# Batch 0's h w2 - h w1 accumulated in PSUM from fp16 weights, w1 w_out made ahead of the first row phase, the full-precision weights loaded behind batch 1's x, and three lines of batch 1's schedule moved

## The chip, the cores and the metric

One core of one Trainium2 chip. The time is the device time of one execution in microseconds (us). "Full clock" below means a mean granted clock of 0.998 to 1.0 over the execution, "low clock" 0.988 to 0.995.

In the lines of the profile PE is TensorE and PEld its weight loads, DVE is VectorE, ACT ScalarE, POOL GpSimd, SP SyncE, and SPq the queue of DMAs that SyncE issues. x9 is a count, and [1.05 <-ACT hwd L474] says that the engine had been idle for 1.05 us until that instruction of ScalarE ended. A chunk is 128 rows of x, an evacuation is the copy of a finished result out of PSUM, a filler is a matmul whose result nobody reads, and a DMA lands when its transfer is complete.

## The reference, cut to what matters

```python
# x: (4, 12544, 128), inducing: (32, 128), w1, w2: (128, 1024), w_out: (1024, 128)
def mab(q, kv):
    s = scale * (q @ kv.transpose(0, 2, 1))
    s = s - s.max(-1, keepdims=True)
    a = np.exp(s)
    a /= a.sum(-1, keepdims=True) + 1e-09
    return a @ kv
h = mab(I, x)            # 32 inducing points look at all 12544 rows, per batch
y = mab(x, h)            # each row looks at the 32 points
# then, per row of y:
g = np.maximum(y @ w1, y @ w2)
out = g @ w_out
```

The kernel uses max(h1, h2) = h1 + relu(h2 - h1). For each batch it therefore needs two small matrices once h is known: hwd = h (w2 - w1), 32 x 1024, which feeds the relus, and m1 = h (w1 w_out), 32 x 128, which feeds the linear part. It needs w1out = w1 w_out for the latter.

## The kernel before

Batch 0 is read and reduced first (the run-up, to about 30 us), because nothing else can start before its h. Then the row phases of batch 0 run, and the pool steps of batch 1 (transposing x, scores, exp, accumulation) are slotted in between, at fixed counts of finished chunks. The same happens for batches 2 and 3.

The weights before: four pieces in full precision, then w1 and w_out in fp16, all in front of x of batch 1 on GpSimd's queue. GpSimd subtracts w1 from w2, which gives w21.

```python
for h in range(2):
    sl = slice(512 * h, 512 * (h + 1))
    nc.gpsimd.dma_start(out=w2f[:, sl], in_=moe_w2[:, sl])
    nc.gpsimd.dma_start(out=w1f[:, sl], in_=moe_w1[:, sl])
nc.gpsimd.dma_start(out=w1h, in_=moe_w1)
nc.gpsimd.dma_start(out=woutp, in_=moe_w_out.rearrange("(jb j) c -> j jb c", j=128))
# ... cut ...
def small_hwd(b, halves=(0, 1)):
    # ... cut: per half of 512 columns ...
    nc.tensor.matmul(out=ps, lhsT=st[b]["hT4"], rhs=w21[:, sl], start=True, stop=True)
    # half 0 is copied by VectorE, half 1 by ScalarE, with rw as the factor for batch 0
```

The end of the run-up, in the order of issue. `fill` issues matmuls on a constant tile; `phase` is one row phase (four matmul groups of 32 rows, then a relu for each); `stage` makes the exp that a block's phases need; weights_2 transposes w1h into w1T (copies by VectorE and ScalarE), weights_3 multiplies w1T and woutp.

```python
for i in range(3):
    load_x(1, i)
weights_1()
weights_1b(nc.gpsimd, slice(512, 1024))
for i in range(3, 7):
    load_x(1, i)
sums = small_h(0)
fill(4)
small_sums(*sums)
stage(blocks[0])
# rw on VectorE
small_hwd(0, (0,))
# ... cut: definitions ...
phase(plan_phase(False))      # first phase
small_hwd(0, (1,))
weights_2()
phase(plan_phase(False))      # second phase
stage(blocks[1])
weights_3()
# ... main loop
```

The schedule of the pool steps. The scores of unit u end in an exp that writes the tile eu; there are NEU = 5 such buffers and 6 units. A DMA transposition on SP's queue (pool_turn) turns eu into eT, and the accumulation reads eT. x itself is transposed into xT on the same queue, in which the stores of the output go too.

```python
t_first, t_step = (8, 2.2) if b == 1 else (-6, 3.4)
for u in range(NU):
    if b == 1:
        s, turn, acc = 24 + 5 * u, 45 + 1.5 * u, 56 + 2 * u
    else:
        s = turn = 9 + 9 * u
        acc = s + 10
    at(base + int(s), pool_scores, b, u)
    at(base + int(turn), pool_turn, b, u)
    at(base + int(acc), pool_accum, b, u)
# ... cut ...
for j in range(14):
    at(base + int(t_first + t_step * j), transpose_x_dma, b, j)
# ... and where a scores or accumulation job may be issued:
late = jobs and chunks_done[0] >= due[jobs[0]] + 4
if jobs and (ck.mode == "col" or len(jobs) > 1 or late):
```

The softmax here doesn't subtract the row's maximum and nothing guards it: scores larger than these inputs give would overflow.

## Time and profile before

| | us |
|---|---|
| median of 3 runs | 337.24 (336.65 to 337.7) |
| the execution that was profiled | 336.5, span 334.4, granted clock 1.000 |
| PE busy | 323.9, 97% of the span |

The median is that of all executions; the profile is one execution. The lines that carry the reading (two stretches in which TensorE waits, 25 to 35 us and 70 to 75 us, in a kernel in which it otherwise hardly waits) are shown in the prediction.

### The profile page before, as it was taken

What the parts mean: (1) busy time and instruction counts of PE and PEld (TensorE: products, weight loads), DVE (VectorE), ACT (ScalarE), POOL (GpSimd) and SP (SyncE); (2) the same over time, 40 slices, a digit from 0 to 9 for tenths busy, and PEclk for the clock granted to TensorE, in tenths of its full rate; (3) what the DMA queues carried; (4) which work ended last, traced back from release to release, by engine and by line L of the source; (5) the groups of instructions that cost most, each with busy time, mean ns of one, the idle gap of its engine ahead of it and who ended that gap; (6) DMA issues with size and microseconds to landing.
All of it is one profiled execution on the core that took longest, in us unless ns stands there. A gap on an engine that the chain in (4) does not pass through costs nothing.

```text
span 334.4 us, 12588 instructions
## 1 busy us (share of the span) xinstructions
PE 323.9 (97%) x5403; PEld 243.5 (73%) x5403; DVE 286.1 (86%) x532; ACT 278.9 (83%) x549; POOL 24.0 (7%) x51
## 2 busy tenths in 40 slices
PE   7987999989999999999999999999999999999995
PEld 3774777757777777777777777777778777777785
DVE  2247999969988999998999999999999989999873
ACT  2558899968688989999888899888879999999961
POOL 7272000000220000000040000000000000000000
PEclk9999999999999999999999999999999999999999
DMA  7999999994299999984279999995222222222233
GB/s 131 211 260 213 200 175 206 204 193 126 64 215 247 245 188 175 167 176 136 84 159 243 237 210 194 187 183 160 86 90 97 82 97 97 86 106 90 77 121 112
DMA packets 70104, 52.93 MB, mean 158 GB/s; under 512 B 52097, under 2 KB 54561, under 8 KB 70049
## 3 DMA queue, kind: packets, MB, share of 16 engines
q1 hardware_dynamic: 64368, 37.71, 47.8%
q0 software_dynamic: 5680, 14.42, 22.1%
q8 instruction: 42, 0.69, 0.9%
q14 instruction: 14, 0.11, 0.1%
HBM read 27.80 MB, written 25.69 MB: 160 GB/s over the span
## 4 chain that ended last, share of the span: by engine, by line
PE 87%; DMA 6%; DVE 2%; ACT 1%; issue 1%; POOL 1%; SPq 1%; DVEq 0%; POOLq 0%; ACTq 0%
PE ps L769 57%; PE ps L930 21%; DMA xn<-in_x_dram 3%; PE ps L574 2%; PE ps L365 2%; PE ps L317 1%; DMA xT<-xn 1%; DVE relu L949 1%; DMA eT<-eu 1%; SPq L171 1%; PE ps L240 1%; POOL xn L165 1%; PE ps L614 1%; PE ps L463 0%; DVE o L796 0%
## 5 line engine op out<-in xcount | busy, mean ns | idle before, releaser
L946 ACT ACTIVATE relu<-ps 128x512 f16<-128x512 f32 x459 | 243.7, 602 | 31.5 <-PE ps L930 23.8
L949 DVE TENSOR_SCALAR relu<-ps 128x512 f16<-128x512 f32 x325 | 208.3, 681 | 21.7 <-PE ps L930 20.2
L769 PE MATMUL ps<-woutp,relu 128*128 128x128 f16 x3136 | 217.9, 220 | 0.0
L769 PEld LDWEIGHTS <-relu 128*128 128x128 f16 x3136 | 177.1, 98 | 39.7 <-issue 29.3
L930 PE MATMUL ps<-e,hwd 32*128 32x512 f16 (+2 forms) x880 | 89.2, 360 | 2.2 <-ACT hwd L474 1.1
L796 DVE TENSOR_TENSOR o<-ps,rp 128x512 f32<-128x512 f32 (+3 forms) x108 | 68.4, 635 | 5.5 <-PE ps L769 3.2
L930 PEld LDWEIGHTS <-hwd 32*128 32x128 f16 x880 | 24.8, 91 | 24.8 <-issue 2.6
L930 PE MATMUL ps<-m,e 32*128 32x128 f16 x381 | 38.8, 217 | 0.8 <-ACT eu L328 0.7
L930 PEld LDWEIGHTS <-e 32*128 32x128 f16 x381 | 21.5, 92 | 3.6 <-issue 0.9
L165 POOL DMA_DIRECT2D xn<-in_x_dram x29 | 15.6, 552 | 3.3 <-POOLq L1120 0.8
L244 DVE COPY xT<-ps 128x1024 f16<-128x1024 f16 (+2 forms) x8 | 5.1, 633 | 9.9 <-PE ps L240 9.9
L328 ACT ACTIVATE eu<-ps 128x512 f16<-128x512 f32 x18 | 10.9, 606 | 3.0 <-DMA eT<-eu 2.4
L247 ACT COPY xT<-ps 128x768 f16<-128x768 f16 (+2 forms) x8 | 5.6, 704 | 8.6 <-PE ps L240 8.6
L586 ACT ACTIVATE e<-ps 128x512 f16<-128x512 f32 (+2 forms) x21 | 11.7, 568 | 0.0
L574 PE MATMUL ps<-xT,hT 128*32 128x512 f16 (+3 forms) x114 | 10.3, 366 | 0.0
L164 POOL COPY pace<-esr 128x1 f32<-128x1 f32 x2 | 0.4, 184 | 137.2 <-DVE esr L399 137.2
L317 PE MATMUL ps<-xT,inducingT 128*32 128x512 f16 x72 | 7.5, 384 | 1.1 <-DMA xT<-xn 1.0
L240 PE MATMUL ps<-identity,xn 128*128 128x128 f16 x98 | 6.8, 220 | 0.1
L365 PE MATMUL ps<-xn,eT 128*32 128x128 f16 x288 | 6.8, 221 | 0.1
L624 DVE RECIPROCAL rp<-ps 128x16 f32<-128x16 f32 (+2 forms) x28 | 6.7, 239 | 0.0
L614 PE MATMUL ps<-ones_q,e 128*128 128x4 f16 x102 | 6.5, 165 | 0.0
L574 PEld LDWEIGHTS <-hT 128*32 128x32 f16 x114 | 2.7, 93 | 5.2 <-issue 4.3
(89 smaller groups left out, 108.5 us busy)
## 6 DMA issues: line engine op xcount, KB each, us to landing
out_dram<-o SPq DMA_DIRECT2D x90, 256.0 KB, 2.5
xn<-in_x_dram POOLq DMA_DIRECT2D x27, 448.0 KB, 10.7
out_dram<-o SPq DMA_DIRECT2D x10, 128.0 KB, 3.7
wf<-in_moe_w_dram POOLq DMA_DIRECT2D x4, 256.0 KB, 12.5
xT<-xn SPq DMA_TRANSPOSE x42, 4.0
out_dram<-o SPq DMA_DIRECT2D x6, 64.0 KB, 5.0
out_dram<-o SPq DMA_DIRECT2D x2, 192.0 KB, 3.0
eT<-eu SPq DMA_TRANSPOSE x18, 2.4
```

The costliest lines, as they stand in the source:

```text
L165: nc.gpsimd.dma_start(out=xn_at[b, i][:, 0:n, :], in_=xr[b, :, k0 : k0 + n, :])
L240: nc.tensor.transpose(ps[:, j, :], xn[:, g + j, :], identity16)
L317: nc.tensor.matmul(out=ps[32 * g : 32 * (g + 1), :], lhsT=inducingT, rhs=xT_tiles[b % 2][:, U * u + 4 * g : U * u + 4 * (g + 1), :], start ...
L328: nc.scalar.activation(out=eu, in_=ps, func=AF.Exp, scale=scale, accum_out=st[b]["es"][:, u : u + 1])
L365: nc.tensor.matmul(out=ps[32 * g : 32 * (g + 1), 0:128], lhsT=eT[:, j, 32 * g : 32 * (g + 1)], rhs=xn_of(b, U * u + 4 * g + j), start=(j = ...
L574: nc.tensor.matmul(out=ps[32 * q : 32 * (q + 1), 128 * t : 128 * (t + n)], lhsT=hq, rhs=xT[:, c : c + n, :], start=True, stop=True, tile_p ...
L586: nc.scalar.activation(out=blk.e2[:, 0 : 128 * wd], in_=ps[:, 0 : 128 * wd], func=AF.Exp, scale=st[0]["rs"] if blk.b == 0 else scale,)
L769: nc.tensor.matmul(out=g.ps[:, 128 * c : 128 * (c + 1)], lhsT=g.blk.relu[q][:, 128 * (jb * w4 + t) : 128 * (jb * w4 + t + 1)], rhs=woutp[: ...
L796: nc.vector.tensor_mul(osb[:, 0:n, :], g.ps[:, 0 : n * C].rearrange("p (s c) -> p s c", s=n), rp)
L930: nc.tensor.matmul(**seq[i])
L946: nc.scalar.activation(out=dst, in_=src, func=AF.Relu)
L949: nc.vector.tensor_scalar(out=dst, in0=src, scalar1=0.0, scalar2=None, op0=ALU.max)
```

## The change

The intent: the first use of hwd needs no subtraction on GpSimd if h w2 and (-h) w1 are summed in PSUM, from fp16 weights: w1 is loaded in fp16 anyway, and one fp16 load of w2 takes the place of the four full-precision pieces ahead of it; then both halves of hwd and w1out are ready when the first phase starts, and the first phases run back to back. The fp32 weights, which the later batches use, move behind x of batch 1. Three lines of the schedule change with it.

```diff
-    wf = relup.tile([128, 2, J], F32, name="wf", tag="relu0")
-    w1f, w2f = wf[:, 0, :], wf[:, 1, :]
+    w2h = relup.tile([128, 4096], F16, name="w2h", tag="relu0")[:, 0:J]
...
-        for h in range(2):
-            sl = slice(512 * h, 512 * (h + 1))
-            nc.gpsimd.dma_start(out=w2f[:, sl], in_=moe_w2[:, sl])
-            nc.gpsimd.dma_start(out=w1f[:, sl], in_=moe_w1[:, sl])
         nc.gpsimd.dma_start(out=w1h, in_=moe_w1)
+        nc.gpsimd.dma_start(out=w2h, in_=moe_w2)
...
+                hTn = smp.tile([C, 4, M], F16, name="hTn_0", tag="hTn", bufs=1)
+                nc.scalar.activation(
+                    out=hTn, in_=st[0]["hps"][:, None, 0:M].broadcast_to((C, 4, M)),
+                    func=AF.Copy, scale=-DOWN,
+                )
...
+                if b == 0:
+                    nc.tensor.matmul(out=ps, lhsT=st[b]["hT4"], rhs=w2h[:, sl], start=True, stop=False)
+                    nc.tensor.matmul(out=ps, lhsT=st[b]["hTn"], rhs=w1h[:, sl], start=False, stop=True)
+                else:
+                    nc.tensor.matmul(out=ps, lhsT=st[b]["hT4"], rhs=w21[:, sl], start=True, stop=True)
...
         def weights_1():
-            nc.gpsimd.tensor_sub(w21[:, 0:512], w2f[:, 0:512], w1f[:, 0:512])
+            # four loads of 512 fp32 columns into x buffers of batch 0 that are free by then
+        def weights_1b():
+            for h in range(2):
+                nc.gpsimd.tensor_sub(w21[:, 512 * h : 512 * (h + 1)], w_of[h][0], w_of[h][1])
...
-        for i in range(3):
+        for i in range(7):
             load_x(1, i)
         weights_1()
-        weights_1b(nc.gpsimd, slice(512, 1024))
-        for i in range(3, 7):
-            load_x(1, i)
         sums = small_h(0)
-        fill(4)
+        weights_2()
         small_sums(*sums)
+        small_hwd(0, (0,))
         stage(blocks[0])
-        small_hwd(0, (0,))
+        small_hwd(0, (1,))
+        weights_3()
...
-            t_first, t_step = (8, 2.2) if b == 1 else (-6, 3.4)
+            t_first, t_step = (6, 2.2) if b == 1 else (-6, 3.4)
-                    s, turn, acc = 24 + 5 * u, 45 + 1.5 * u, 56 + 2 * u
+                    s, turn, acc = 25 + 5 * u, 45 + 1.5 * u, 55 + 2 * u
-            late = jobs and chunks_done[0] >= due[jobs[0]] + 4
+            late = jobs and (chunks_done[0] >= due[jobs[0]] + 4 or jobs[0][1][1] == NU - 1)
...
         phase(plan_phase(False))
-        small_hwd(0, (1,))
-        weights_2()
         phase(plan_phase(False))
         stage(blocks[1])
-        weights_3()
+        weights_1b()
```

(The diff is cut, and two bodies are condensed to a comment; the moved line that makes rw is left out.)

More of the change, by code (lines that the diff above doesn't have):

```diff
@@ L433, in small_h @@
                 ready = ck.on_act(st[0]["end"], 0.2)
+                hTn = smp.tile([C, 4, M], F16, name="hTn_0", tag="hTn", bufs=1)
+                nc.scalar.activation(
+                    out=hTn,
+                    in_=st[0]["hps"][:, None, 0:M].broadcast_to((C, 4, M)),
+                    func=AF.Copy,
+                    scale=-DOWN,
+                )
+                st[0]["hT4r"] = ck.on_act(0.0, 0.3)
+                st[0]["hTn"] = hTn.rearrange("c q m -> c (q m)")
                 st[b]["hT4"] = hT4.rearrange("c q m -> c (q m)")
@@ L452, in small_sums @@
             nc.vector.reciprocal(out=st[0]["rs"], in_=ps[:, 2:3])
-            ck.bank[st[0]["eb"]] = st[0]["rsr"] = ck.on_dve(end, 0.17)
+            nc.vector.tensor_scalar(out=st[0]["rw"], in0=st[0]["rs"], scalar1=1.0 / scale, scalar2=None, op0=ALU.mult)
+            ck.bank[st[0]["eb"]] = st[0]["rsr"] = ck.on_dve(end, 0.34)
         def small_hwd(b, halves=(0, 1)):
@@ L462, in small_hwd @@
                 ck.wait(max(ck.bank[bi], st[b]["hT4r"]), "p1")
-                nc.tensor.matmul(out=ps, lhsT=st[b]["hT4"], rhs=w21[:, sl], start=True, stop=True)
-                end = ck.run(0.215)
+                if b == 0:
+                    nc.tensor.matmul(out=ps, lhsT=st[b]["hT4"], rhs=w2h[:, sl], start=True, stop=False)
+                    nc.tensor.matmul(out=ps, lhsT=st[b]["hTn"], rhs=w1h[:, sl], start=False, stop=True)
+                    end = ck.run(0.43)
+                else:
+                    nc.tensor.matmul(out=ps, lhsT=st[b]["hT4"], rhs=w21[:, sl], start=True, stop=True)
+                    end = ck.run(0.215)
                 if half == 0:
@@ L501, in weights_1 @@
         def weights_1():
-            nc.gpsimd.tensor_sub(w21[:, 0:512], w2f[:, 0:512], w1f[:, 0:512])
-        def weights_1b(eng, sl):
-            eng.tensor_sub(w21[:, sl], w2f[:, sl], w1f[:, sl])
+            for h in range(2):
+                sl = slice(512 * h, 512 * (h + 1))
+                wf = [xn_tiles[3 + 2 * h + n].rearrange("p k c -> p (k c)")[:, 0:1024].bitcast(F32) for n in (0, 1)]
+                nc.gpsimd.dma_start(out=wf[0], in_=moe_w2[:, sl])
+                nc.gpsimd.dma_start(out=wf[1], in_=moe_w1[:, sl])
+                w_of[h] = wf
+        def weights_1b():
+            for h in range(2):
+                nc.gpsimd.tensor_sub(w21[:, 512 * h : 512 * (h + 1)], w_of[h][0], w_of[h][1])
         def weights_2():
@@ L665 @@
         p1_accum(0, 7)
-        for i in range(3):
+        for i in range(7):
             load_x(1, i)
         weights_1()
-        weights_1b(nc.gpsimd, slice(512, 1024))
-        for i in range(3, 7):
-            load_x(1, i)
         sums = small_h(0)
-        fill(4)
+        weights_2()
         small_sums(*sums)
+        small_hwd(0, (0,))
         stage(blocks[0])
-        nc.vector.tensor_scalar(out=st[0]["rw"], in0=st[0]["rs"], scalar1=1.0 / scale, scalar2=None, op0=ALU.mult)
-        small_hwd(0, (0,))
+        small_hwd(0, (1,))
+        weights_3()
         blocks[0].staged = max(blocks[0].staged, st[0]["hwdr"])
```

## The prediction

> **What bounds the kernel now.** I read the page first, then the busy time in stretches of 5 us, and went into the two stretches that stand out with the timeline, the waits and the DMA queue of SP.
>
> The page, busy time and share of the span:
>
> ```profile
> PE 323.9 (97%) x5403; PEld 243.5 (73%) x5403; DVE 286.1 (86%) x532; ACT 278.9 (83%) x549; POOL 24.0 (7%) x51
> ```
>
> TensorE is the bound as an average, with the two engines that empty PSUM close behind. The change keeps the stream of matmuls (10,786 PE rows become 10,778), so a gain can only come from stretches in which TensorE waits. Stretches (us from the span's start; then busy us of PE, PEld, DVE, ACT, POOL, clock, DMA share, GB/s):
>
> ```profile
> 25.00:30.00 5.00, 3.73 (x57) 2.26 (x58) 3.76 (x9) 4.02 (x8) 1.96 (x5) 1.00 1.07 210
> 30.00:35.00 5.00, 4.57 (x67) 2.92 (x66) 4.01 (x8) 4.76 (x10) 0.00 (x0) 1.00 1.08 216
> 35.00:40.00 5.00, 5.00 (x81) 3.69 (x80) 4.97 (x10) 4.39 (x9) 0.00 (x0) 1.00 1.06 225
> ...
> 70.00:75.00 5.00, 3.35 (x46) 2.23 (x43) 2.92 (x5) 2.53 (x7) 0.00 (x0) 1.00 0.80 233
> 75.00:80.00 5.00, 4.99 (x94) 3.64 (x92) 4.20 (x9) 4.32 (x10) 0.00 (x0) 1.00 0.39 107
> ```
>
> There are two holes: the run-up (25 to 35 us, 1.7 us of PE idle and 14 filler matmuls besides) and one around 70 to 75 us (1.65 us). From 95 to 320 us PE is busy 224.87 of 225 us, so what is gained earlier is kept.
>
> The run-up, from the timeline (start, length, engine, line):
>
> ```profile
> 24.12 0.75 DVE L467 TENSOR_SCALAR hwd<-ps,rw 128x512 f16<-128x512 f32 x1 [0.30 <-PE ps L463]
> ...
> 24.92 0.40 PE L930 MATMUL ps<-e,hwd 32*128 32x128 f16 x9 [0.85 <-DVE hwd L467]
> ...
> 26.39 0.69 ACT L474 ACTIVATE hwd<-ps,rw 128x512 f16<-128x512 f32 x1
> 26.58 0.41 DVE L516 COPY w1T<-ps 128x512 f16<-128x512 f16 x1
> ...
> 26.96 0.60 ACT L519 COPY w1T<-ps 128x512 f16<-128x512 f16 x1
> 27.14 0.40 PE L930 MATMUL ps<-e,hwd 32*128 32x128 f16 x9 [1.05 <-ACT hwd L474]
> ```
>
> The first row phase starts at 24.92, the second only at 27.14, because the second half of hwd goes through ACT behind two relus; w1T is copied in the same place, and the third phase starts at 29.66.
>
> The second hole, from the waits between 60 and 76 us (who waited for whom: total, times, longest), and the DMA queue of SP:
>
> ```profile
> ACT eu L328 <- DMA eT<-eu: 2.4, 1, 2.4
> ...
> PE ps L317 <- DMA xT<-xn: 1.0, 1, 1.0
> PE ps L930 <- ACT eu L328: 0.7, 1, 0.7
> ```
>
> ```profile
> 66.32 2.92 SPq L171 DMA_TRANSPOSE xT<-xn  x1
> 69.33 1.01 SPq L821 DMA_DIRECT2D out_dram<-o  x2
> 70.43 2.54 SPq L354 DMA_TRANSPOSE eT<-eu  x2
> ```
>
> The sixth eu reuses the buffer of the first, so ACT waits until the first eT transposition has read it (issued at 70.43, landed at 73.05), and ACT's relus stand behind. SP issues without a gap from 41.99 to 70.43: 14 xT transpositions (10 of about 1.28 us, 4 of 1.85 to 2.9) and 9 stores. A store held at 69.33 has had its data since 64.6. So this queue, in order, is late, not the data.
>
> **What the Trainium skill says.** "TensorE: Matmul & The Clock Gate", Back-to-back issue gap, gives N/2.4 + 2.5 ns warm, 216 ns for 512 columns. The trace agrees: four overlapping 512-column phase matmuls take about 0.33 us of the chain, and the 128-column ones 0.056 us each. So the two extra 512-column matmuls cost some 0.22 us each. "PSUM — Partial Sum Buffer", The four PSUM rules: a matmul without the first-flag adds where the bank was written before; so h w2 - h w1 needs no subtraction on an engine, only the negated hTn. The trace before uses that in its accumulations. "DMA: Bandwidth & Descriptors", Queues, rings and completion order: each DMA engine takes turns between the queues, by packet; so early transpositions share the engines with x of batch 1. The trace agrees in that a 64 KB store issued at 31.12, beside the loads of x, landed after 6.6 us, against a median of 5.0 for its kind. "SBUF — State Buffer", on the shared port pair: GpSimd's two-input subtraction locks out VectorE operations in a 2-port mode or with two SBUF inputs. The relus read PSUM, so moving the 1.28 and 1.26 us of subtraction beside them should cost nothing; no row before shows that directly.
>
> **The change part by part.**
>
> Loads. Before, behind x of batch 0 (landed 19.97 by the landing records) came four fp32 pieces, 21.26 to 23.34, w1h 24.35, woutp 25.78, x of batch 1 27.91 to 41.55. After, w1h and w2h take about 1.0 us each (w1h took 24.35 - 23.34 = 1.01) and woutp 1.43: 21.0, 22.0, 23.4. x of batch 1 lands 2.4 us earlier, and the fp32 pieces (0.63 each, 2.5) end near 41.7. All weights are there before the accumulation ends at 22.66, except woutp, wanted only at about 24.7.
>
> Up to the first phase. Eight w1h transposes (0.45) stand where four fillers were: 22.72 to 23.17. es at 22.99 as before; then L448 takes 0.3, to 23.5. hTn on ACT is one more instruction of about 0.28 (I choose the DVE twin's 0.29): 23.05 to 23.35, beside the transposes. hwd half 0: two matmuls, 0.43, to 23.95 (end 24.1); DVE 24.15 to 24.9, its w1T copy (0.41) fitting before rs. Stage 0.33, exp on ACT 0.45 after its start: 24.40 to 25.09. hwd half 1 on PE to 24.75, eight w1T*woutp matmuls (0.45) to 25.2. So the first phase starts at about 25.2, 0.3 later than now.
>
> After it. hwd half 1 on ACT is done at about 25.75, so the second phase is at 25.8 against 27.14: 1.3 earlier. Not all of that is kept. ACT now has five relus (2.7 us) ahead of the exp of block 1, which ends near 29.1 against 29.25 now, and the third phase waits for it: 29.15 against 29.66. The sounder account is by work: DVE and ACT lose, after the first phase, w1T 0.41 + 0.60, hwd half 1 0.69 and w1out 0.28 = 1.98 us, about 1.0 per engine, less the 0.3 of the later first phase. Both bind up to 42 us, so I take **0.8 us** (0.5 to 1.3).
>
> The hole at 70. The listing of the order shows the first xT transposition ahead of the fourth store instead of behind it, and the last one store earlier in the queue; T0 runs at about 36.6 and T1 at about 41.2 (behind the fourth store, whose data came at 41.6, now 0.8 earlier) against 43.42. From there as many transpositions and stores lie ahead of the first eT as before, 27.0 us: issue at 68.2, landing 70.8 against 73.05. The last xT lands near 69, when PE asks for it at about 69.2. ACT is ready for the sixth eu at about 69.9, so a wait of 0.9 is left of 2.45. PE lost about 2.4 us here (69.54 to 74.21 holds 2.3 us of its usual work); of the 2.1 that ACT's wait can give back beyond the shift, I take **1.2 us** (0 to 2.1).
>
> The rest: two filler matmuls less, four relus moved from DVE (681 ns) to ACT (602 ns), two pool steps of batch 3 a dozen finals sooner: 0 +/- 0.2. Sum 2.0 us: 337.24 - 2.0 = 335.2; I state 335.1, as the relus' shift leans to gain.
>
> **The rivals.** (1) ACT takes the place of hwd: the early phases pile relus on ACT and only 0.3 us remains; for it speaks 4.76 of 5 us busy at 30 to 35. With no gain at 70: 336.9. (2) The SP queue is no sooner: transpositions beside x and fp32 loads take longer, and the eT lands as late as now. For it, 6.6 us for the store at 31.12; against it, the loads end by 41.7, where they ended before. Then only the run-up counts: 336.4. (3) The hole closes entirely, as the eT is held only by its store's data (67.68 less 0.8): 0.8 + 2.1 = 2.9, 334.3. (4) woutp late, or a DMA hiccup like x's fifth tile (3.53 us where others took 2.1): the eight matmuls ahead of the first phase would hold everything; up to 1 us lost, 336.2.
>
> **Range and chances.** The rivals span 334.3 to 336.9; the three times before spread 1.05. I give 333.9 to 336.6. Two per cent is 6.7 us, over twice all that the two holes hold, and nothing found costs as much: within 2% is nearly sure.
>
> **What would show it.** Right: first phase at 24.9 to 25.5 and second within 0.8 of it; no ACT hwd copy between relus; third phase at 28.7 to 29.4; the first eT issued before 69 and the wait of L317 for xT gone; PE busy over 4.3 us in the stretch 70 to 75 or the one before. Wrong: a first phase after 26 (weights late), an eT still issued near 70, or a new wait of SP or of ACT between 40 and 75. POOL's subtraction beside relus longer than 0.69 us would say that the port matters.

## The result, and the profile after

| | before | after |
|---|---|---|
| median of 6 runs, same rounds | 337.51 (336.65 to 338.21) | 335.04 (333.61 to 335.81) |
| ratio | | 0.9921 (0.9893 to 0.995) |

A ratio here is the mean time of one kernel's runs over that of the other's of the same rounds, so it is not quite the ratio of the medians quoted. The result is within 2%, a gain of 2.5 us, and the predicted 335.1 lies 0.06 us from the median. The agreement is better than the reasoning was, as will be seen.

The busy time on the page after (the line that answers to the one the prediction shows of before):

```profile
PE 325.6 (98%) x5399; PEld 245.1 (73%) x5399; DVE 284.4 (85%) x528; ACT 280.3 (84%) x554; POOL 24.6 (7%) x52
```

PE became 1.7 us *busier* with fewer instructions. That does not come from the change: another execution of the same kernel (a_again, below) has 323.7. The timeline of the run-up after (start, length, engine, line):

```profile
24.21 0.75 DVE L478 TENSOR_SCALAR hwd<-ps,rw 128x512 f16<-128x512 f32 x1
...
25.12 0.68 ACT L485 ACTIVATE hwd<-ps,rw 128x512 f16<-128x512 f32 x1
25.40 0.85 PE L946 MATMUL ps<-e,hwd 32*128 32x128 f16 x18
...
25.90 2.55 ACT L962 ACTIVATE relu<-ps 128x512 f16<-128x512 f32 x5
...
29.08 0.37 PE L946 MATMUL ps<-e,hwd 32*128 32x512 f16 x1 [1.00 <-ACT e L604]
```

(Line numbers moved: the row phase's L930 is L946 now, its relus L962 and L965, the scores L313, their exp L324.) Eighteen matmuls in one group at 25.40 are the first and second phase back to back (before: nine at 24.92 and nine at 27.14). ScalarE's hwd copy is now ahead of its relus, and the third phase is at 29.08 against 29.66. So far this is what was predicted, to 0.2 us. But now the same stretches in windows of 3.41 us (us; PE, PEld, DVE, ACT, POOL busy; granted clock; DMA share; GB/s):

```profile
26.03:29.44 3.41, 2.07 (x37) 1.17 (x30) 2.42 (x6) 3.41 (x7) 1.00 (x2) 1.00 1.07 213
29.44:32.86 3.42, 3.16 (x31) 1.87 (x29) 2.05 (x4) 2.88 (x7) 0.62 (x2) 0.50 1.06 212
32.86:36.27 3.41, 3.41 (x37) 2.61 (x35) 2.64 (x6) 1.64 (x4) 0.00 (x0) 0.50 1.08 217
36.27:39.68 3.41, 3.41 (x58) 2.66 (x57) 2.97 (x6) 3.12 (x7) 0.00 (x0) 1.00 1.04 301
```

From 29.44 to 36.27 the granted clock is 0.50: PE is busy throughout 32.86:36.27 with 37 instructions, and throughout the next window with 58. A granted clock of 0.989 as an average over 334 us hides 6.83 us at one half. The profiled execution of the kernel before had no such stretch (clock 1.000), so the two pages cannot be subtracted from each other as they stand.

The second hole, in the waits between 60 and 76 us (who waited for whom; total, times, longest), and the windows of 5 us there:

```profile
DVE relu L965 <- PE ps L946: 1.0, 2, 0.5
DVE o L812 <- PE ps L785: 0.9, 1, 0.9
ACT relu L962 <- PE ps L946: 0.7, 2, 0.4
```

```profile
70.00:75.00 5.00, 5.00 (x84) 3.78 (x81) 4.50 (x8) 4.35 (x12) 0.00 (x0) 1.00 0.63 176
```

Both waits for a DMA (ScalarE's eu for eT, TensorE's scores for xT) are gone, and PE is busy 5.00 of 5 us against 3.35.

**A ledger.** To see where time was gained, I numbered the 108 evacuations of output (VectorE, `o<-ps,rp`) in each trace and took, for the same number, the start before minus the start in the other trace: how many us sooner that kernel is there. Evacuation 3 (40.91 us before) closes the run-up, 15 (77.96) the second hole, 57 (200.66) lies behind the arrival of batch 3's x, 107 is the end.

| trace | clock | at 3 | at 15 | at 57 | at 80 | at the end |
|---|---|---|---|---|---|---|
| after | 0.989 | -1.09 | 1.26 | 0.94 | 0.52 | 0.49 |

In the throttled trace the run-up *loses* 1.09, and the second hole gives 2.35. The experiments ask for the parts of that, at full clock. The theories, in short: (T) the two gains are those of the prediction, and the throttle hides one of them; (R) the weights' part is worth little, and the schedule numbers bring what is left; and, for the hole, (Q) SP's late queue alone against (S) the order of the scores, or both.

### The profile page after: what moved, and what is told of

It reads as the page before. It is cut to its first block, busy times and chain, and to the rows that moved or that the text cites. A ratio compares the mean times of both kernels' runs of the same rounds, so it can differ in the third digit from the quotient of the medians.

```text
span 333.9 us, 12581 instructions
## 1 busy us (share of the span) xinstructions
PE 325.6 (98%) x5399; PEld 245.1 (73%) x5399; DVE 284.4 (85%) x528; ACT 280.3 (84%) x554; POOL 24.6 (7%) x52
## 4 chain that ended last, share of the span: by engine, by line
PE 92%; ACT 3%; DVE 2%; DMA 1%; SPq 1%; issue 1%; DVEq 0%
PE ps L785 57%; PE ps L946 21%; PE ps L592 2%; PE ps L236 2%; PE ps L361 2%; PE ps L313 2%; PE ps L658 1%; DMA xT<-xn 1%; ACT xT L243 1%; ACT relu L962 1%; DVE relu L965 1%; SPq L171 1%; PE ps L632 1%; PE ps L252 1%; DVE o L812 0%
## 5 line engine op out<-in xcount | busy, mean ns | idle before, releaser
L962 ACT ACTIVATE relu<-ps 128x512 f16<-128x512 f32 x463 | 245.1, 602 | 33.9 <-PE ps L946 27.1
L965 DVE TENSOR_SCALAR relu<-ps 128x512 f16<-128x512 f32 x321 | 205.9, 680 | 22.2 <-PE ps L946 20.8
L946 PE MATMUL ps<-e,hwd 32*128 32x512 f16 (+2 forms) x880 | 89.7, 364 | 1.3 <-ACT e L604 1.0
L946 PEld LDWEIGHTS <-hwd 32*128 32x128 f16 x880 | 25.2, 91 | 22.3 <-issue 2.3
L946 PE MATMUL ps<-m,e 32*128 32x128 f16 x381 | 39.1, 218 | 0.0
L946 PEld LDWEIGHTS <-e 32*128 32x128 f16 x381 | 21.4, 93 | 3.6 <-issue 1.0
L324 ACT ACTIVATE eu<-ps 128x512 f16<-128x512 f32 x18 | 10.9, 608 | 0.5 <-PE ps L313 0.4
L313 PE MATMUL ps<-xT,inducingT 128*32 128x512 f16 x72 | 7.2, 385 | 0.4 <-DMA xT<-xn 0.4
```

The source lines that it names most:

```text
L313: nc.tensor.matmul(out=ps[32 * g : 32 * (g + 1), :], lhsT=inducingT, rhs=xT_tiles[b % 2][:, U * u + 4 * g : U * u + 4 * (g + 1), :], start ...
L324: nc.scalar.activation(out=eu, in_=ps, func=AF.Exp, scale=scale, accum_out=st[b]["es"][:, u : u + 1])
L946: nc.tensor.matmul(**seq[i])
L962: nc.scalar.activation(out=dst, in_=src, func=AF.Relu)
L965: nc.vector.tensor_scalar(out=dst, in0=src, scalar1=0.0, scalar2=None, op0=ALU.max)
```

## The experiments

Beside the time, each experiment's trace is entered in the ledger; the whole of it stands at the end of this section. All runs were correct. Times are medians, with the ratio to the kernel before in the same rounds. They went in three groups of four, each group on one chip with its own runs of the kernel before: 337.69 (336.47 to 338.19) for the first four below, 337.42 (336.0 to 338.21) for the second four, 337.6 (336.6 to 338.05) for the last four.

**a_again: the changed kernel, unaltered.** No edit.

> The changed kernel unaltered, as a control. If the granted clock of TensorE is what makes its times spread (333.6 and 333.9 us with a mean clock of 1.000, 335.7 and 335.8 with 0.988 to 0.989), the new runs fall into the same groups: about 333.8 us at clock 1.000, 335 to 336 at 0.995 or less. If the spread has nothing to do with the clock, times and clocks do not go together. The kernel before is expected at 337.4 with clock 1.000 in every run.

333.85 us (333.6 to 334.7), 0.9898 (0.9863 to 0.9932). Its trace fell at clock 1.0: run-up +1.13, hole another 2.36, but only 2.14 left at the end. So the throttle cost the first trace 2.2 us (1.13 + 1.09) in the run-up. The same stretch in this trace:

```profile
25.00:30.00 5.00, 3.60 (x63) 2.41 (x61) 3.26 (x9) 4.90 (x10) 1.12 (x3) 1.00 1.06 210
30.00:35.00 5.00, 4.78 (x72) 3.28 (x70) 4.62 (x10) 4.90 (x11) 0.54 (x1) 1.00 1.07 213
```

**b_fill: sixteen filler matmuls ahead of the third phase.** The planner's clock is put back, so that no other instruction moves.

```diff
         def phase(jobs):
+            state["phases"] = state.get("phases", 0) + 1
+            if state["phases"] == 1 and "started" in state:
+                pe0 = ck.pe
+                fill(16)
+                ck.pe = pe0
...
+        state['phases'] = 0
+        state['started'] = True
```

> The changed kernel with 16 filler matmuls (0.9 us) in the wait of TensorE of 1.0 us ahead of the third row phase, nothing else altered. Theory: that wait, in a stretch that is idle anyway, lets the clock fall to half; then every run here has a mean clock of 1.000 and about 333.7 us, a ratio near 0.989 to before. Rival: the clock falls for another reason; then some runs still show 0.988 to 0.995 and 335 to 336 us, with a mean near 335.

333.04 us (332.58 to 333.27), 0.9869 (0.9842 to 0.9895), and all four executions at clock 1.0. The fillers only use time in which PE waits for the exp of block 1:

```profile
26.82:30.23 3.41, 3.26 (x58) 2.36 (x52) 2.28 (x7) 3.41 (x8) 1.08 (x2) 1.00 1.07 213
```

PE is busy 3.26 of 3.41 us where it was busy 2.07. The run-up gains 1.18 as in a_again, so the fillers cost nothing.

**c_sched: the kernel before with the three schedule numbers only.**

```diff
-            t_first, t_step = (8, 2.2) if b == 1 else (-6, 3.4)
+            t_first, t_step = (6, 2.2) if b == 1 else (-6, 3.4)
-                    s, turn, acc = 24 + 5 * u, 45 + 1.5 * u, 56 + 2 * u
+                    s, turn, acc = 25 + 5 * u, 45 + 1.5 * u, 55 + 2 * u
-            late = jobs and chunks_done[0] >= due[jobs[0]] + 4
+            late = jobs and (chunks_done[0] >= due[jobs[0]] + 4 or jobs[0][1][1] == NU - 1)
```

> The kernel before with the schedule numbers of the change alone (first xT transposition two chunks sooner, scores and sums of batch 1 moved by one, the last sum never held back); weights as before. Theory of the prediction: the hole at 70 us is late because the DMA queue of SP is late, so this part alone closes most of it: 1.2 to 2.4 us less, 335.0 to 336.2, with clock 1.000. Rival: x of batch 1, which lands 2.4 us sooner only with the new order of weights, is needed for it: then no gain, 337 us.

335.88 us (334.94 to 336.78), 0.9954 (0.9917 to 0.9991); clocks 1.0, 0.994, 0.99, 0.99. Ledger: 0.00 in the run-up, 2.36 in the hole. With the schedule's lines the weights add nothing at 70 us, to the hundredth.

**d_weights: the changed kernel with those three lines put back.** The diff is c_sched's, reversed.

> The changed kernel with the schedule numbers of before: the weights' part alone. Theory: only the run-up gains, 0.6 to 0.8 us in runs with clock 1.000 (336.7), and nothing or a loss in runs with a lower clock (337 to 338); the wait of ACT for the first eT near 70 us stays. Rival: the run-up and the earlier x close the hole too: 335 or less.

335.41 us (334.86 to 336.79), 0.9947 (0.9913 to 0.998), all at clock 1.0. Ledger: 1.35 in the run-up, 0.24 in the hole. The weights' part brings no more than that to the hole; ScalarE's wait for eT is still 2.2 us there. And there is no loss between evacuations 57 and 80, which a_again, b_fill and c_sched all have.

**e_tfirst: the kernel before with t_first alone, 8 to 6.** This is the step on which the prediction's 1.2 us rested: SP's queue sooner, nothing else.

```diff
-            t_first, t_step = (8, 2.2) if b == 1 else (-6, 3.4)
+            t_first, t_step = (6, 2.2) if b == 1 else (-6, 3.4)
```

> The kernel before with one number altered: xT transpositions of batch 1 two chunks sooner. Every engine's order stays as it was, only the DMA queue of SP has another. If the hole at 70 us is the late queue alone, the first eT is issued about 1.8 us sooner (68.7 instead of 70.43), the wait of PE for xT (1.0 us) goes, and the evacuation of the store after the hole is some 1.8 to 2.4 us sooner than before, as in the run with all schedule numbers (2.36). Rival: that gain comes also from where scores and eu stand among the relus (the other numbers); then a rest of the wait of ACT stays and the gain is 1 to 1.8 us.

336.1 us (335.88, 336.31; both at full clock), 0.9966 (0.992 to 1.0013). Ledger: 0.44 in the hole, not 1.2 or more. The waits between 60 and 76 us:

```profile
ACT eu L328 <- DMA eT<-eu: 2.0, 1, 2.0
...
PE ps L930 <- ACT eu L328: 1.3, 1, 1.3
```

The wait of the scores for xT is gone, and in exchange PE waits 1.3 instead of 0.7 us for ScalarE, which is still held by eT. Its queue issued the first eT at 69.66, 0.77 sooner than before; it landed at 72.67, 0.38 sooner. The queue's order up to there is that of c_sched, which issued it at 68.66. Among what differs are two stores that took longer to issue, here 1.97 and 1.44 us, in c_sched 0.53 and 0.39; the first of them here, then in c_sched:

```profile
58.92 1.97 SPq L821 DMA_DIRECT2D out_dram<-o  x1
```

```profile
58.53 0.53 SPq L821 DMA_DIRECT2D out_dram<-o  x1
```

The data of that store had been ready since 55.49, so this is no wait for data. The 0.44 is therefore one trace's reading of the sooner queue, and not the most that it can give.

**f_before_fill: the kernel before with 8 fillers ahead of the first phase and 14 ahead of the second.**

```diff
         small_hwd(0, (0,))
+        pe0 = ck.pe
+        fill(8)
+        ck.pe = pe0
...
         weights_2()
+        pe0 = ck.pe
+        fill(14)
+        ck.pe = pe0
```

> The kernel before with fillers in its two waits of TensorE in the run-up (8 ahead of the first phase, 14 ahead of the second), nothing else altered. In five of seven runs of the last call the kernel before had a clock of 0.989 to 0.994 and 337.6 to 338.2 us, in two 0.998 to 0.999 and 336.5. If its clock falls because of the run-up, all runs here have 1.000 and about 336.4. If it falls elsewhere (the hole at 70 us, the end), the same mix of 0.99 and 1.00 stays.

336.35 us (334.54 to 336.56), 0.9956 (0.9911 to 1.0001); all four at 0.999 or 1.0, while of the kernel before's seven runs five were at 0.989 to 0.994. The ledger is flat at -0.05 to -0.06. So fillers do nothing for an execution at full clock (336.47 is the median of before's own full-clock runs); they only keep it from the low one. (The 334.54 is 2 us from the other three at the same clock, and d_weights has one at 336.79 against 334.86; neither was traced, and the cause is open.)

**g_late1: b_fill, with the new "late" rule for batch 1 only.**

```diff
-            late = jobs and (chunks_done[0] >= due[jobs[0]] + 4 or jobs[0][1][1] == NU - 1)
+            late = jobs and (chunks_done[0] >= due[jobs[0]] + 4 or jobs[0][1] == (1, NU - 1))
```

> The changed kernel with the fillers, and the rule for the last sum of a batch (never held back) kept for batch 1 alone. The ledger of evacuations showed 0.45 us lost between 230 and 260 us in the three kernels that have the rule and none in the one without. If the rule costs it, the loss is gone and the time is 332.6, 0.4 below the 333.04 of the kernel with fillers. If not, 333.0.

332.47 us (331.94 to 332.87), 0.9858 (0.9825 to 0.989). The ledger has 3.41 at 15, 3.26 at 57, 3.26 at 80 and at the end: the 0.42 us that every kernel with the full rule loses between 57 and 80 is gone.

**h_early3: g_late1, with batch 3's transpositions six chunks sooner.**

```diff
-            t_first, t_step = (6, 2.2) if b == 1 else (-6, 3.4)
+            t_first, t_step = (6, 2.2) if b == 1 else (-6, 3.4) if b == 2 else (-12, 3.4)
```

> As the last, with the xT transpositions of batch 3 six chunks sooner; only the order of SP's queue differs. Between 193 and 200 us single traces lost or won 0.3 to 0.9 us by when xT landed. If that is the same illness as in batch 1, this loss goes in every run: 331.5 to 332.5 and a narrower spread. If the transpositions only wait for x and hold the stores, nothing or a loss: 332.6 to 333.5.

334.18 us (333.96 to 334.51), 0.991 (0.988 to 0.9941): worse than g_late1 by 1.7. The DMA queue of SP in that stretch:

```profile
183.78 5.05 SPq L171 DMA_TRANSPOSE xT<-xn  x1
188.92 0.54 SPq L837 DMA_DIRECT2D out_dram<-o  x1
```

A transposition takes 5.05 us to issue, while the last loads of batch 3's x are still under way (the last landed at 189.13), and the stores wait behind it. It was not held by its own data, which had landed at 171.52; what held it the trace does not say. The ledger drops from 3.61 at 57 to 2.18 at 62, and the timeline of TensorE shows where:

```profile
205.50 0.41 PE L361 MATMUL ps<-xn,eT 128*32 128x128 f16 x16 [1.35 <-DMA eT<-eu]
```

With more transpositions of x ahead of it in the queue, batch 3's first eT is issued at 201.45 and lands at 205.46; in g_late1 it was 198.35 and 200.69, and TensorE did not wait for it.

**i_scores: c_sched with t_first left at 8**, so the numbers of the scores and the rule without the sooner queue.

```diff
-                    s, turn, acc = 24 + 5 * u, 45 + 1.5 * u, 56 + 2 * u
+                    s, turn, acc = 25 + 5 * u, 45 + 1.5 * u, 55 + 2 * u
-            late = jobs and chunks_done[0] >= due[jobs[0]] + 4
+            late = jobs and (chunks_done[0] >= due[jobs[0]] + 4 or jobs[0][1][1] == NU - 1)
```

> The kernel before with the other half of the schedule numbers: scores and sums of batch 1 moved by one chunk and the rule for the last sum; the DMA queue of SP in its old order. The transpositions alone gave 0.43 us at the hole at 70 us, both together 2.36. If the moved scores do it alone (eu 5 comes to ACT behind three more relus, when the eT has landed anyway): 1.9 to 2.4 us at the evacuation after the hole. If it takes both (with late transpositions the last scores wait for xT): under 1.4 us, and a wait of PE for xT of 1 us is left.

336.46 us (335.62 at clock 0.999, 337.3 at 0.995), 0.9972 (0.993 to 1.0015). The trace is the low-clock one (0.5 from 28.03 for 3.41 us, run-up -1.20), so only the hole is read from it: 1.00. The waits between 60 and 76 us:

```profile
ACT eu L328 <- DMA eT<-eu: 1.7, 1, 1.7
...
PE ps L317 <- DMA xT<-xn: 1.0, 1, 1.0
```

Both waits are still there. In these single traces the queue alone gives 0.44, the scores alone 1.00, both together 2.36. That is not a sum to be relied on, as the queue's own speed differs by about 1 us between executions of one order; what is shown is that either part alone leaves a wait and both together leave none.

**j_wlate: the changed kernel with weights_2 and weights_3 back in their old places**, both halves of hwd still ahead of the first phase.

```diff
         sums = small_h(0)
-        weights_2()
+        fill(4)
...
         small_hwd(0, (1,))
-        weights_3()
...
         phase(plan_phase(False))
+        weights_2()
         phase(plan_phase(False))
         stage(blocks[1])
+        weights_3()
```

> The changed kernel with w1T and w1*w_out made where they were before (after the first and the second phase), hwd still from two matmuls ahead of the first phase. Account by work: w1T and w1out are 1.29 of the 1.98 us that the change takes out of the stretch after the first phase, so 0.65 us of the run-up gain (1.12 us at the third evacuation) should go, less up to 0.3 that the earlier first phase gives back: gain 0.5 to 0.8 left. Rival: the second half of hwd, which held the second phase, is the whole gain: 1.1 us stays.

333.8 us (333.63, 333.96), 0.9893 (0.9862 to 0.9925). The second phase is nearly as soon, yet the run-up's ledger is -0.05: no gain at all. (The time does not show it, since this trace gains 0.52 near 200 us, where a_again's loses 0.90.) The timeline of the phases:

```profile
26.33 0.68 PE L945 MATMUL ps<-e,hwd 32*128 32x128 f16 x9
29.94 0.39 PE L945 MATMUL ps<-e,hwd 32*128 32x512 f16 x1 [0.76 <-DVE m L501]
```

The third phase waits for m1, which VectorE makes from w1out, which was made from w1T; that chain starts only after the first phase here. My expectation that 0.5 to 0.8 us would be left was wrong.

**k_wfirst: the changed kernel with the fp32 loads in front of batch 1's x again.**

```diff
+        weights_1()
         for i in range(7):
             load_x(1, i)
-        weights_1()
```

> The changed kernel with the fp32 weights loaded ahead of x of batch 1 as before; engines' orders are the same, only GpSimd's queue differs. x of batch 1 lands some 2.5 to 4 us later. If the sooner x was worth nothing, the evacuations stay within 0.1 us of the changed kernel's at full clock (1.12 us sooner than before at the third, 3.49 after the hole). If the transpositions then wait for x, the hole comes back in part: 1 to 2 us less after it.

335.78 us (335.51 at 0.989, 336.06 at 1.0), 0.9952 (0.9919 to 0.9985). Its trace is throttled just like the first one of the changed kernel (0.5 for 6.83 us from 29.06), so those two may be compared: -1.09 and 1.27 against -1.09 and 1.26, although x of batch 1 lands from 31.41 to 45.68 here and from 26.25 to 39.45 there. An earlier x of batch 1 is worth nothing. (The time of its full-clock run, 336.06, is 2.4 above the changed kernel's; one run, and the trace does not explain it. It stays open.)

**l_stage1: g_late1 with the exp of block 1 between the first and second phase.**

```diff
         phase(plan_phase(False))
-        phase(plan_phase(False))
         stage(blocks[1])
+        phase(plan_phase(False))
```

> The best version so far (changed kernel, fillers, rule for batch 1 alone: 332.47 us) with block 1 staged between the first and the second phase, so that its exp on ACT comes ahead of three relus and the third phase is not held until 29.08. If ACT's order is what holds the third phase, it starts near 28.4 and 0.3 to 0.6 us are won: 332.0. If the two evacuating engines are simply full there, the relus come later by what the exp comes sooner: 332.5.

332.38 us (332.29 to 333.58), 0.9862 (0.9831 to 0.9893): the same as g_late1. The third phase is at 29.19, the run-up's ledger 1.10. With the exp out of the way (it ends at 27.61 here) the third phase is no sooner: VectorE finishes m, which that phase reads, at 28.97, and the fillers ahead of it run to 29.14. What it would gain without the fillers was not tried; by m it could be 0.2 at most.

The whole ledger (us sooner than the kernel before's trace):

| trace | clock | at 3: run-up | at 15 | so in the hole | at 57 | at 80 | end |
|---|---|---|---|---|---|---|---|
| after | 0.989 | -1.09 | 1.26 | 2.35 | 0.94 | 0.52 | 0.49 |
| a_again | 1.000 | 1.13 | 3.49 | 2.36 | 2.59 | 2.17 | 2.14 |
| b_fill | 1.000 | 1.18 | 3.53 | 2.35 | 4.04 | 3.62 | 3.59 |
| c_sched | 1.000 | 0.00 | 2.36 | 2.36 | 2.06 | 1.64 | 1.61 |
| d_weights | 1.000 | 1.35 | 1.59 | 0.24 | 1.29 | 1.28 | 1.28 |
| e_tfirst | 1.000 | -0.06 | 0.38 | 0.44 | 0.19 | 0.20 | 0.20 |
| f_before_fill | 0.999 | -0.05 | -0.05 | 0.00 | -0.06 | -0.06 | -0.06 |
| g_late1 | 0.999 | 1.06 | 3.41 | 2.35 | 3.26 | 3.26 | 3.26 |
| h_early3 | 0.999 | 1.19 | 3.54 | 2.35 | 3.61 | 2.17 | 2.17 |
| i_scores | 0.995 | -1.20 | -0.20 | 1.00 | -0.24 | -0.67 | -0.70 |
| j_wlate | 0.999 | -0.05 | 2.30 | 2.35 | 2.82 | 2.40 | 2.37 |
| k_wfirst | 0.989 | -1.09 | 1.27 | 2.36 | 1.18 | 0.75 | 0.73 |
| l_stage1 | 1.000 | 1.10 | 3.45 | 2.35 | 3.96 | 3.96 | 3.95 |

## Why the prediction was right, and where only its sum was

**The run-up (predicted 0.8, range 0.5 to 1.3).** Right in mechanism and nearly in size: 1.06 to 1.35 in the six full-clock traces that have it (a_again, b_fill, d_weights, g_late1, h_early3, l_stage1). Phase times came as stated (25.40, second right behind, third 29.08), although x of batch 1 began to land only 1.7 us sooner (26.25 against 27.91), not 2.4; k_wfirst shows that this did not matter. The two matmuls of a half of hwd start 0.22 us apart (23.56 and 23.78), the cost that was put on each. Two points were too generous or too mean. The text named hwd's second half first; j_wlate shows that moving it sooner gains nothing unless w1T and w1out go ahead too, because m1 then ends last. And the account by work (1.98 us off two engines, less 0.3) gave 0.7, taken as 0.8, some 0.3 to 0.6 short of what was measured; which term is short the runs do not separate. The loads were put too short as well (w2h took 1.5 us after w1h, in a_again 2.0, not 1.0), so x came less early; no engine waited for it.

**The hole at 70 us (predicted 1.2, range 0 to 2.1).** This is the step that was mis-sized: 2.35 or 2.36 measured, in every trace with the whole schedule. The prediction let ScalarE be ready for the sixth eu at 69.9 and the first eT land at 70.8, which left a wait of 0.9. ScalarE's timeline before, then the DMA queue of SP and ScalarE's timeline in the full-clock trace of the changed kernel (a_again):

```profile
73.16 0.60 ACT L328 ACTIVATE eu<-ps 128x512 f16<-128x512 f32 x1 [2.45 <-DMA eT<-eu]
```

```profile
67.01 3.02 SPq L350 DMA_TRANSPOSE eT<-eu  x2
```

```profile
68.86 1.58 ACT L962 ACTIVATE relu<-ps 128x512 f16<-128x512 f32 x3 [0.38 <-PE ps L946]
70.31 0.62 ACT L324 ACTIVATE eu<-ps 128x512 f16<-128x512 f32 x1
...
70.88 0.62 ACT L324 ACTIVATE eu<-ps 128x512 f16<-128x512 f32 x1
```

The first eT is issued at 67.01 (predicted 68.2, before 70.43) and landed at 70.23; the fifth and sixth eu stand side by side behind three relus, so the sixth is wanted at 70.88, when its buffer is free. Before, it was wanted at about 70.7 and freed only at 73.05. Nothing was left to wait for.

The term that failed is ScalarE's readiness. The prediction moved it with the run-up alone, and did not count that the scores themselves had been moved: six relus now stand between the fourth eu and the fifth, where four stood. c_sched, which has no shift from the run-up, separates the two terms. Its first eT lands at 71.39, 1.66 sooner than before, and its sixth eu is wanted at 72.01, 1.3 later. Together that is more than the 2.45 of the wait; either alone would leave some of it, as e_tfirst (2.0) and i_scores (1.7) do. So "the SP queue is late" was a right reading, worth an estimated 1.7 with c_sched's queue times and 0.44 in e_tfirst's, and the other half is the order of the scores.

That the first eT would be issued "before 69" failed in the throttled trace (70.28), where everything ahead of it ran later, and held in a_again and in c_sched (68.66). In the throttled trace it landed at 73.02, 0.09 before the sixth eu began. Which of s, acc and the rule does it within the scores' half was not tried one by one. Rival 3, the hole closing entirely, was the right one. Its reason, an eT held only by its store's data, fits too: the store just ahead of it was issued at 66.58 in a_again and 67.71 in c_sched, when its evacuation had ended at 66.56 and 67.68. The order of the scores it did not have.

**The rest (predicted 0 +/- 0.2).** Wrong. The prediction read PE's 224.87 busy of 225 us from 95 to 320 as a sign that an earlier gain is kept; part of it was not. (Its count of PE rows, 10,786 and 10,778, is in no kept trace; the pages have 5403 and 5399 matmuls.) The "late" rule, written for any batch, also takes 0.42 us between 200 and 266 us, in batch 3: all seven traces with the full rule lose 0.41 to 0.43 there, all six without it or with it for batch 1 alone lose nothing, but for h_early3's wait for eT. And between 100 and 200 us the ledger moves by -0.90 to +0.52 from execution to execution of kernels that are equal there (a_again -0.90, after -0.32, b_fill +0.51). All of it comes at one evacuation, number 57, at 196 to 201 us. In a_again the timeline shows TensorE waiting for batch 3's transposed x:

```profile
193.89 0.39 PE L313 MATMUL ps<-xT,inducingT 128*32 128x512 f16 x2 [0.25 <-DMA xT<-xn]
194.68 0.38 PE L313 MATMUL ps<-xT,inducingT 128*32 128x512 f16 x1 [0.40 <-DMA xT<-xn]
```

What makes those transfers later in one execution than in another is open.

**The port shared by GpSimd and VectorE.** The prediction held that the subtraction beside relus would cost nothing, and said that relus over 0.69 us would refute it. The subtractions ran at 41.23 and 42.69 for 1.27 us each; relus of VectorE that began beside them, at 41.41 and 42.77, took 0.68 and 0.63. That agrees, on two relus; the subtractions themselves took 1.28 and 1.26 before.

**The base.** The prediction compared everything with 337.24, and took the profile, an execution of 336.5 at full clock, for what lies behind that number. Most executions are not like it. Of the kernel before's 21 runs in the experiments' three groups:

| | full clock | low clock |
|---|---|---|
| before | 336.47, median of 5 | 337.7, median of 16 |
| after and a_again, 10 runs | 333.61, median of 5 | 335.08, median of 5 |

The change is worth 2.9 us at full clock and 2.6 at low. The forecast of 335.1 falls on the median because four of the six runs behind that median had a low clock (335.0 to 335.81; the other two took 333.61 and 333.92). So errors in it offset each other: a hole mis-sized by 1.2 on one side, a state of the clock that it did not know of and the losses behind 100 us on the other. That the number was met to 0.06 us is luck.

**The clock.** The Trainium skill, "TensorE: Matmul & The Clock Gate", What's actually happening, says that the clock is halved after an idle window, that windows last 3413 ns and run freely. The traces agree on the size: the drops lasted 3.41 us (i_scores) and 6.83 (after, k_wfirst), one and two windows, and in all three traces the drop began 23.89 us, seven windows, after the clock had first been released. That first release was at 3.97 to 7.05 us in the different traces, so the windows lie differently over the same instructions in different executions. That alone does not make the two kinds: in after and a_again, one kernel, the windows lie alike to 0.01 us and the phases to 0.1 us, PE is busy 2.07 and 2.08 us in the window from 26.03 and 26.02, and only the first dropped. The traces do not agree that a window must be idle. The page names a second pattern in A second HAM failure mode (many small idle times between groups), and this is nearer: in the windows ahead of the drops PE was busy 1.58 (i_scores), 2.01 (k_wfirst) and 2.07 us (after) of 3.41. But no sharp threshold follows from it, for these two kept the full clock:

```profile
26.02:29.44 3.42, 2.08 (x36) 1.22 (x36) 2.51 (x6) 3.42 (x7) 1.08 (x2) 1.00 1.08 214
```

```profile
23.36:26.77 3.41, 1.94 (x25) 1.00 (x24) 2.41 (x6) 1.97 (x4) 3.41 (x6) 1.00 1.28 210
```

The first is a_again's, the second e_tfirst's. The windows here are the same 3.41 us ones, counted from the first release. In the fourteen traces, up to 80 us, none with 2.13 us or more dropped, the one at 1.58 did, and those from 1.94 to 2.08 went either way. Where fillers raised the lowest of those between 19 and 40 us to 2.9 us or more (b_fill, f_before_fill, g_late1, h_early3, l_stage1), all 20 runs were at 0.998 or more. Shown is that fillers avoid the drop; what exactly the hardware counts is open. d_weights had no low run in four either, nor e_tfirst and j_wlate in two each, without fillers, which with half of a_again's and after's runs low may be luck.

**A better version.** g_late1 and l_stage1, the changed kernel with sixteen fillers and the rule for batch 1 alone, ran at 332.47 and 332.38, 0.986 of the kernel before against 0.9921 and 0.9898 for the changed kernel in its two sets of rounds (different ones, so the two are compared only by way of the kernel before).

## What to carry to other kernels

Before you subtract two profiles, compare their mean granted clocks to the third digit, and look for a short stretch at one half: 0.989 was worth 2.2 us here, as much as the whole forecast. Where an engine is held by two waits in series, taking one away shows you the other; price both, try the parts alone and together, and ask both when a buffer comes free and when it is wanted, since the change here moved both ends of one wait. And a rule that is written for one stage and coded for all of them deserves a trace of the other stages: this one paid 0.4 us back in batch 3.

## What the Trainium skill lacked or had wrong

- "TensorE: Matmul & The Clock Gate": it ties the return to half clock to an idle window, and Why this matters for your kernels to gaps of over about 3 us. Here it happened with no gap of TensorE longer than 1.05 us in the windows ahead, with PE busy 1.58, 2.01 and 2.07 of 3.41 us, and not after others with 1.94 and 2.08. What share of activity is enough is not stated, and busy time in the profile does not decide it between 1.94 and 2.08.
- The same page does not mention filler matmuls as a remedy; here 16 to 22 of them, of 128 columns, in time that PE waited anyway, kept the clock in 20 of 20 runs (five kernels), where the kernel before dropped in 16 of 21 and the changed one in 5 of 10.
- "DMA: Bandwidth & Descriptors" has the time that a transposition by DMA takes in the issuing sequencer only in a comparison made for trn3, and no page has its spread on this chip. Here most took about 1.28 us, 9 to 13 of the 42 in each trace over 1.4 and up to 3.2, and one beside the loads of x 5.05 (h_early3), with the stores behind it held. A store, mostly 0.3 to 0.5 us to issue, took 1.97 once with its data ready (e_tfirst).
